# Making GpSimd's loads wait for the preceding DMA transposes, in a sliding-window attention followed by a SiLU MLP

## The chip, the cores and the metric

The kernel runs on one core of a Trainium2 chip. The metric is device time in microseconds (us), median of several executions. An execution over 1.5% above the fastest of its kernel is called slow, the others fast. Ratios use fast executions alone; medians are over all. A profile is one execution. Its times count from the start of its span.

## The reference, cut to what matters

```python
# q, k, v: (8 batches, 8 heads, 576 positions, 64), float32
scores = q @ k.T / 8
# heads 0-3: plain window of 32 positions; heads 4-7: every 4th of 128
attn = softmax(where(mask, scores, -1e9))
x = (attn @ v) -> (4608 tokens, 512)
h = x @ w_in                    # 512 -> 2048
out = (h * sigmoid(h)) @ w_out  # 2048 -> 512
```

The MLP takes most of TensorE's time: 9 groups of 512 tokens, each with a part `h` (x times w_in) and a part `y` (times w_out). A group needs the attention of one more batch than the group before it (the last group excepted).

## The kernel before

Batches 0 and 1 are transposed on TensorE. For batches 2 to 7, the route of q and k is: GpSimd issues a DMA that casts them to fp16 in DRAM (`kq_s`, `issue_cast`); SyncE issues four DMA transposes that read `kq_s` and write `nat` (heads 0-3) and `kqT` (heads 4-7) in SBUF (`issue_turn`; the four for batch b are called "step b" below); TensorE makes the scores; the attention output goes to DRAM (`x_s<-oP`, `x_s<-oD`, SyncE) and comes back through one more DMA transpose (`xA<-x_s` or `xR<-x_s`, SyncE) as the input of `h`. The output stores (`out_dram<-ob`; `ob` is a buffer that `y` is copied to) are in SyncE's queue as well. GpSimd also loads v (`vraw`, `vp`).

```python
def issue_cast(b):                       # GpSimd queue
    for i, src in enumerate((k, q)):
        nc.gpsimd.dma_start(out=kq_s[b][i]..., in_=src[b]...)

def issue_turn(b):                       # SyncE queue: "step b"
    ...
    for i in range(2):                   # nat: overlapping windows, 2304 x 128
        nc.sync.dma_start_transpose(out=dst[:, None, :], in_=win)
    for i in range(2):                   # kqT
        nc.sync.dma_start_transpose(out=kqTs[b % 2][:, i], in_=rows)

def issue_v(b):                          # GpSimd queue: vraw twice, vp once
    ...

def turn_gen(b):
    issue_turn(b)
    yield "DMA", max(12.0, ARRIVE.get(b, (0.0,))[0] - plan.now)

def group_gen(g):
    ...
    nc.sync.dma_start_transpose(out=x_of(g)[:, :, GT - n :], in_=x_s[t0 : t0 + n])
    yield "DMA", 6.0

# in attention(b):
if kind == "S" and b + 2 < B:            # after the last scores of batch b: step b + 2
    st.after = lambda: count(("S", b), NS,
        lambda: plan.push(turned[b + 2], turn_gen(b + 2), plan.t))
if kind in "PD":                         # after the last attn @ v of batch b
    def loads():
        if b + 2 < B: issue_v(b + 2)
        if b + 3 < B: issue_cast(b + 3)
    st.after = lambda: count(("V", b), NB + 2 * DIL, loads)
```

The program is put in order at build time by a small planner (`plan`). The numbers in `yield "DMA", us` and in `ARRIVE` are its guesses of when data will be there. They delay nothing on the chip; they only shape the order of instructions in each engine's queue. Each queue runs in order.

The softmax here doesn't subtract the row's maximum and nothing guards it: scores larger than these inputs give would overflow.

## Time and profile before

| before | |
|---|---|
| time | 400.66 us, median of 2 runs (399.76 to 401.56) |
| PE busy | 310.9 us of 399.8, 78% |
| PE busy in 260-400 us | 39.7 of 40, then 95.9 of 100 us |
| PE busy in 66-102 us | 7.5 of 36 us |
| PE busy in 160-190 us | 9.4 of 30 us |

The profile page: busy time per engine, then the span in 40 slices of 10 us. A digit is the busy share in tenths. PEclk is the clock granted to TensorE in tenths, GB/s is what the DMA engines moved.

```profile
span 399.8 us, 5645 instructions
PE 310.9 (78%) x2200; PEld 148.8 (37%) x2200; DVE 200.4 (50%) x477; ACT 153.4 (38%) x258; POOL 45.7 (11%) x64
PE   0679985060898099900999499999999999999996
PEclk9999999557799689975799979999999999999999
GB/s 118 192 201 206 192 161 151 85 162 89 196 205 207 153 35 133 127 92 190 21 153 179 176 128 180 147 84 58 78 67 59 126 75 26 26 54 26 28 79 79
```

PE has holes at slices 7-10, 13-14, 18-19 and 23 (counted from 1), and is full from slice 24, 230 us, on. So TensorE is the limit late in the kernel, and something else is the limit early. The waits view says what ended each idle stretch (columns: who waited and for whom, us in total, times, longest us):

```profile
PE h L602 <- DMA xR<-x_s: 26.9, 2, 20.7
ACT ob L641 <- DMA out_dram<-ob: 23.1, 2, 15.9
PE s L402 <- DMA nat<-kq_s: 17.6, 1, 17.6
PE y L630 <- ACT ob L641: 11.1, 2, 10.9
PE h L602 <- DMA xA<-x_s: 9.6, 1, 9.6
```

PE's four lines add up to 65 us. Every one ends with a DMA that SyncE issues: a step (`nat`), an x transpose, or an output store that frees `ob`. SyncE's timeline, cut to steps 2 and 4 and what follows them (start us, duration us, merged instructions with their count; a merged line covers the waits in it):

```profile
50.71 23.83 SPq L130 DMA_TRANSPOSE nat<-kq_s  x2
74.58 12.03 SPq L134 DMA_TRANSPOSE kqT<-kq_s  x2
86.66 0.58 SPq L642 DMA_DIRECT2D out_dram<-ob  x1
...
113.53 13.72 SPq L130 DMA_TRANSPOSE nat<-kq_s  x2
127.35 2.89 SPq L134 DMA_TRANSPOSE kqT<-kq_s  x2
130.34 2.69 SPq L475 DMA_DIRECT2D x_s<-oD  x2
136.87 1.44 SPq L297 DMA_TRANSPOSE xA<-x_s  x1
```

A step holds the queue for 36 us (50.7 to 86.6) or 17 us (113.5 to 130.2). What stands behind it goes out at its end: the first output store at 86.66, the last stores of batch 2's attention at 130.34. Only then can `xA` be transposed, and `h` of group 2 starts at 140.3.

Why is a step so slow? The DMA view of the stretch 68-80 us, in the middle of step 2 (q1 is SyncE's queue, q0 GpSimd's; packets, MB, share of 16 engines' time; times of packets overlap, so shares can add to over 100%):

```profile
DMA packets 4361, 1.08 MB, mean 90 GB/s; under 512 B 3918, under 2 KB 4361, under 8 KB 4361
q1 hardware_dynamic: 2155, 0.55, 99.4%
q0 software_dynamic: 2206, 0.54, 81.5%
```

Two queues share the engines, about equally in bytes, and together move 90 GB/s. The same view of 20-28 us, when only GpSimd's queue moves data:

```profile
DMA packets 2235, 1.62 MB, mean 202 GB/s; under 512 B 62, under 2 KB 2233, under 8 KB 2233
```

And of 216-220 us, when nearly only transposes run:

```profile
DMA packets 3597, 0.91 MB, mean 228 GB/s; under 512 B 3565, under 2 KB 3597, under 8 KB 3597
```

### The profile page before, as it was taken

The page shows a single profiled execution, that of the slowest core. Times are in us where ns is not written, and L with a number is a line of the kernel's source. Part 1 is how long each engine was busy: PE and PEld are TensorE (multiplying, and loading weights), DVE is VectorE, ACT ScalarE, POOL GpSimd, SP SyncE. Part 2 cuts the span into 40 slices and gives each one's busy share as a digit, 9 for nine tenths or more (in the row PEclk, how much of TensorE's full clock was granted, in tenths as well). Part 3 has the DMA queues.
Part 4 walks back from the last instruction along what each step waited for, and adds up shares of the span by engine and source line. Part 5 has one row for each costly group of instructions (what it writes and reads, how often), then busy time and mean ns, then how long its engine had stood idle before and what let it go on. Part 6 is the DMA issues. An engine that isn't in the chain of part 4 may idle for free.

```text
span 399.8 us, 5645 instructions
## 1 busy us (share of the span) xinstructions
PE 310.9 (78%) x2200; PEld 148.8 (37%) x2200; DVE 200.4 (50%) x477; ACT 153.4 (38%) x258; POOL 45.7 (11%) x64
## 2 busy tenths in 40 slices
PE   0679985060898099900999499999999999999996
PEld 0553443020343044400444144444444444444442
DVE  6584696020687058600585358577568625425300
ACT  1554750000555055500455144544555425435311
POOL 8525312000020011000020010000000000000000
PEclk9999999557799689975799979999999999999999
DMA  9999999999999919998099949621311610010022
GB/s 118 192 201 206 192 161 151 85 162 89 196 205 207 153 35 133 127 92 190 21 153 179 176 128 180 147 84 58 78 67 59 126 75 26 26 54 26 28 79 79
DMA packets 115898, 47.41 MB, mean 119 GB/s; under 512 B 82592, under 2 KB 111264, under 8 KB 115872
## 3 DMA queue, kind: packets, MB, share of 16 engines
q0 software_dynamic: 47152, 19.92, 43.3%
q1 hardware_dynamic: 68720, 27.14, 40.9%
q8 instruction: 17, 0.28, 0.3%
q14 instruction: 9, 0.07, 0.1%
HBM read 39.84 MB, written 20.05 MB: 150 GB/s over the span
## 4 chain that ended last, share of the span: by engine, by line
PE 64%; DMA 12%; SPq 11%; DVE 8%; ACT 2%; issue 1%; POOL 1%; ACTq 0%; POOLq 0%
PE h L602 29%; PE y L630 28%; SPq L134 6%; SPq L130 5%; DMA out_dram<-ob 4%; DMA x_s<-oD 3%; DMA xR<-x_s 3%; PE s L402 2%; DMA nat<-in_q_dram 2%; DVE oD L442 2%; PE av_d L438 2%; DVE gT L613 2%; DVE oP L442 1%; PE av_p L438 1%; DVE probs L417 1%
## 5 line engine op out<-in xcount | busy, mean ns | idle before, releaser
L630 PE MATMUL y<-w_out,gT 128*128 128x512 f16 x576 | 142.7, 387 | 11.7 <-ACT ob L641 11.1
L613 DVE SCALAR_TENSOR_TENSOR gT<-th,h 128x512 f16<-128x512 f32 x144 | 98.1, 683 | 89.9 <-ACT th L611 89.8
L611 ACT ACTIVATE th<-h 128x512 f32<-128x512 f32 x144 | 86.1, 598 | 121.6 <-PE h L602 114.4
L602 PE MATMUL h<-xR,w_in 128*128 128x512 f16 x384 | 95.5, 389 | 26.9 <-DMA xR<-x_s 26.9
L602 PEld LDWEIGHTS <-w_in 128*128 128x128 f16 x576 | 54.9, 100 | 101.8 <-issue 48.4
L630 PEld LDWEIGHTS <-gT 128*128 128x128 f16 x576 | 54.4, 99 | 73.5 <-issue 15.8
L602 PE MATMUL h<-xA,w_in 128*128 128x512 f16 x192 | 51.1, 401 | 11.4 <-DMA xA<-x_s 9.6
L410 ACT ACTIVATE probs<-s 128x768 f16<-128x768 f32 (+2 forms) x45 | 36.4, 808 | 35.6 <-PE s L402 35.6
L641 ACT ACTIVATE ob<-y 128x512 f32<-128x512 f32 x36 | 21.5, 598 | 69.0 <-PE y L630 45.9
L438 PEld LDWEIGHTS <-probs 128*128 128x128 f16 x448 | 23.6, 102 | 15.4 <-issue 1.5
L417 DVE TENSOR_TENSOR probs<-probs,mask_p 128x768 f16<-128x768 f16 x24 | 13.3, 553 | 31.3 <-ACT probs L410 30.9
L442 DVE TENSOR_TENSOR oD<-av_d,rcps 72x256 f16<-72x256 f32 x64 | 26.9, 421 | 2.2
L441 DVE RECIPROCAL rcps<-av_p 96x4 f32<-96x4 f32 x48 | 8.4, 175 | 36.9 <-PE av_p L438 36.6
L140 POOL DMA_DIRECT2D vraw<-in_v_dram x16 | 10.9, 681 | 110.1 <-DVE vd L429 93.2
L442 DVE TENSOR_TENSOR oP<-av_p,rcps 96x256 f16<-96x256 f32 x48 | 20.2, 421 | 1.6
L402 PE MATMUL s<-nat 64*128 64x96 f16 x144 | 7.0, 224 | 17.6 <-DMA nat<-kq_s 17.6
L154 POOL DMA_DIRECT2D vp<-in_v_dram x8 | 11.5, 1436 | 70.7 <-PE av_p L438 65.6
L438 PE MATMUL av_d<-vd,probs 128*128 128x65 f16 x256 | 16.4, 199 | 1.0 <-DVE rcps L441 0.6
L438 PE MATMUL av_p<-vp,probs 128*128 128x65 f16 x192 | 13.8, 205 | 1.5 <-DVE probs L417 0.9
L417 DVE TENSOR_TENSOR probs<-probs,mask_d 128x864 f16<-128x864 f16 (+1 forms) x24 | 13.2, 549 | 1.7 <-ACT probs L410 1.4
L402 PEld LDWEIGHTS <-nat 64*128 64x128 f16 x144 | 4.2, 103 | 25.9 <-issue 25.9
L372 PE MATMUL td<-ident,nat 96*128 96x96 f16 x48 | 4.3, 242 | 11.1 <-DMA nat<-in_k_dram 7.0
(59 smaller groups left out, 117.2 us busy)
## 6 DMA issues: line engine op xcount, KB each, us to landing
out_dram<-ob SPq DMA_DIRECT2D x36, 256.0 KB, 2.7
kq_s<-in_k_dram POOLq DMA_DIRECT2D x6, 576.0 KB, 18.6
kq_s<-in_q_dram POOLq DMA_DIRECT2D x6, 576.0 KB, 21.0
vp<-in_v_dram POOLq DMA_DIRECT2D x7, 384.0 KB, 14.5
w_in<-in_moe_w_in_dram POOLq DMA_DIRECT2D x4, 512.0 KB, 12.4
w_out<-in_moe_w_out_dram POOLq DMA_DIRECT2D x4, 512.0 KB, 16.5
vraw<-in_v_dram POOLq DMA_DIRECT2D x8, 224.0 KB, 9.0
x_s<-oP SPq DMA_DIRECT2D x12, 144.0 KB, 2.7
```

Source lines behind the costliest of these rows:

```text
L130: nc.sync.dma_start_transpose(out=dst[:, None, :], in_=win)
L134: nc.sync.dma_start_transpose(out=kqTs[b % 2][:, i], in_=rows)
L402: nc.tensor.matmul(sp[i][:, w * n : w * (n + 1)], lhs, rhs, start=True, stop=True)
L410: nc.scalar.activation(p2, both[:, :, :n], AF.Exp, scale=scale)
L417: nc.vector.tensor_tensor(p2, p2, mk, ALU.mult)
L438: nc.tensor.matmul(a[:, i, : D + 1], lhs(i), rhs(i), start=True, stop=True)
L442: nc.vector.tensor_tensor(o, a[:n, :, :D], rcp[:n, :, None].broadcast_to([n, HN, D]), ALU.mult)
L602: nc.tensor.matmul(h, w_in16[:, c, f * P : (f + 1) * P], x_g[:, c], start=(c == 0), stop=(c == HP - 1),)
L611: nc.scalar.activation(th, h, AF.Tanh, scale=0.5)
L613: nc.vector.scalar_tensor_tensor(gTs[g][:, f], th, 1.0, h, ALU.add, ALU.mult)
L630: nc.tensor.matmul(y, gTs[g][:, f, tb * P : (tb + 1) * P], w_out16[:, f], start=(f == 0), stop=(f == NFF - 1),)
L641: nc.scalar.activation(ob, y, AF.Copy, scale=0.5)
```

## The change

Its intent is to keep the loads of v and the casts out of the way of the transposes. Two GpSimd copies read the last column of each `kqT` of step b. GpSimd's queue runs in order, so the loads behind these copies are issued only when the step has landed. Steps 2 and 3 are also given later planned times, and a few guesses of the planner are changed.

```diff
+    fence = cpool.tile([P, 2], F16, name="fence")
...
-    ARRIVE = {0: (8.5, 15.0), 1: (33.0, 47.0), 2: (60.0, 60.0), 3: (75.0, 75.0)}
+    ARRIVE = {0: (8.5, 15.0), 1: (33.0, 47.0), 2: (60.0, 70.0), 3: (80.0, 90.0)}
+    TURN_AT = {2: 51.0, 3: 72.0}
...
     def turn_gen(b):
+        yield "DMA", max(0.0, TURN_AT.get(b, 0.0) - plan.now)
         issue_turn(b)
-        yield "DMA", max(12.0, ARRIVE.get(b, (0.0,))[0] - plan.now)
+        count(("L", b - 2), 2, lambda: loads_after(b))
+        yield "DMA", 9.0
+
+    def loads_after(b):
+        for i in range(2):
+            nc.gpsimd.tensor_copy(fence[:, i : i + 1], kqTs[b % 2][:, i, 1, HN * M - 1 :])
+        issue_v(b)
+        if b + 1 < B:
+            issue_cast(b + 1)
...
-        yield "DMA", 6.0                     # group_gen
+        yield "DMA", 8.0
...
-                def loads():
-                    if b + 2 < B:
-                        issue_v(b + 2)
-                    if b + 3 < B:
-                        issue_cast(b + 3)
-
-                st.after = lambda: count(("V", b), NB + 2 * DIL, loads)
+                if b + 2 < B:
+                    st.after = lambda: count(
+                        ("V", b), NB + 2 * DIL,
+                        lambda: count(("L", b), 2, lambda: loads_after(b + 2)),
+                    )
```

## The prediction

> **What bounds the kernel now.** TensorE, but only after about 230 us. Page: PE busy 310.9 us of 399.8. Windows view: PE busy 29.6 of 30 us in 230-260, 39.7 of 40 in 260-300, 95.9 of 100 in 300-400; that tail can't shrink. The loss is earlier. The waits view lists five PE waits ended by a DMA or by what one held up: `s<-nat` 17.6 us (to 83.6), `y` behind `ob`, whose buffer waits for an output store, 10.9 (to 101.5), `h<-xA` 9.6 (to 140.3), `h<-xR` 20.7 (to 190.1) and 6.2 (to 230.4). Together 65 us.
>
> **Their cause.** SyncE's timeline shows the four transposes of a step taking, first issue to last, 36 us (step 2), 21, 17, 31, 18, then 12 (step 7). Nothing later in that queue can start before them: the x_s<-oD stores of the batch two earlier go out at 130.3, 180.9 and 220.8, within 0.1 us of a step's last transpose. The slow steps are those with GpSimd's v loads and casts in flight. DMA view: alone, casts move about 200 GB/s (20-28 us), transposes 228 (216-220); together 90 (68-80) and 99 (88-100). The Trainium skill, "DMA: Bandwidth & Descriptors", section "Issuing engines are not separate DMA queues", says queues interleave on the same 16 DMA engines; the trace agrees, and adds that the sum halves.
>
> **What the change does.** Two tiny GpSimd copies per step (estimate 0.1-0.3 us each, from the other small GpSimd instructions; off the critical path) read the transposes' last column, so v(b) and casts(b+1) start only when step b has landed. Transposes 2 and 3 move back in SyncE's queue. No byte is saved.
>
> Estimates: 1.77 MB of transposes per step at 220 GB/s plus landing, 10 us. 1.95 MB (v and casts) at 200 GB/s plus issue and landing, 16 us (15 at 199-214). They now alternate, 27 us per step, less than TensorE's 35.
>
> Casts 2 land at 53.5 as before, so transposes 2 land near 62, casts 3 near 78, transposes 3 near 88, casts 4 near 104-108; transposes 4 finish near 114-120 (130.2 before). What follows collides: x_s<-oD and the x transpose now always run against the just released v and casts. At the 40-60 GB/s that transposes got in company, that adds about 7 us to the 9.5 seen from last transpose to `h`. Group 2's `h` starts near 131 (140.3 before), group 3's near 160-167 (190.1), group 4's near 195-205 (230.4); the remaining 169.5 us follow unchanged. Of 65 us of waits 30-35 remain: 20-30 before group 2, where TensorE has run out of work, and small ones later.
>
> **Predicted: 366 us, 8 in 10 between 350 and 384.** Faster by over 2%: 0.92; within 2%: 0.05; slower by over 2%: 0.03.
>
> **What would show it right.** Each step's transposes take 8-13 us of SyncE's queue, with neither v nor casts in flight. `s<-nat` waits under 5 us, `h<-xR` under half of 26.9; `h<-xA` stays or grows (10-30). New: GpSimd waits for kqT. PE is dense from about 205 us; its busy time falls a little (300-310), with fewer restarts at a low granted clock.
>
> **What would make it wrong.** Output stores stuck behind a transpose that waits for its later casts, stalling `y`: the alternation is a serial chain and can pass 30 us per step. x transposes slowed by over 7 us. Or an x path less disturbed than I think: then near 354. A late step 7 starving groups 5 or 6.

## The result, and the profile after

The kernel after takes 354.0 us (median of 2 runs, 353.42 to 354.58). The ratio to the kernel before is 0.8835 (95% interval 0.873 to 0.894). A ratio here is the mean time of one kernel's fast runs over that of the other's in the same rounds, so not quite the ratio of the medians. Run again later with five rounds, it took 354.1 us (ratio 0.8953, 0.890 to 0.901).

The page after (slices are 8.8 us now):

```profile
span 352.8 us, 5672 instructions
PE 305.7 (87%) x2200; PEld 148.0 (42%) x2200; DVE 201.7 (57%) x477; ACT 153.5 (44%) x258; POOL 48.2 (14%) x76
PE   0678998992987199789998999999999999999995
PEclk9999999997899579989999999999999999999999
GB/s 111 188 205 201 196 190 201 128 192 187 194 199 142 165 233 197 151 163 86 210 156 224 235 172 144 19 123 41 87 64 149 61 0 30 61 30 30 61 82 67
```

PE's work is the same 2200 matmuls. Two holes (slices 10 and 14, counted from 1) are left of four, and PE is nearly full from slice 19, 160 us, on. The waits view after, the same kinds of line:

```profile
POOL fence L300 <- DMA kqT<-kq_s: 142.8, 12, 31.6
PE h L611 <- DMA xA<-x_s: 10.2, 1, 10.2
ACT ob L650 <- DMA out_dram<-ob: 9.8, 1, 9.8
PE y L639 <- ACT ob L650: 8.1, 5, 6.6
PE h L611 <- DMA xR<-x_s: 4.3, 2, 3.2
```

The wait of `s` for `nat` (17.6 us) is gone; `h` for `xR` fell from 26.9 to 4.3; PE's lines add up to 22.6 us instead of 65. These 43 us and the 5 us by which PE's busy time fell (310.9 to 305.7) account for about the 47 us by which the span fell. GpSimd now idles 142.8 us at the fence, which costs nothing in itself: what it holds back there is the loads, as meant. SyncE's timeline after, the same places:

```profile
49.77 6.33 SPq L131 DMA_TRANSPOSE nat<-kq_s  x2
56.15 2.90 SPq L135 DMA_TRANSPOSE kqT<-kq_s  x2
59.10 0.58 SPq L651 DMA_DIRECT2D out_dram<-ob  x1
...
98.87 5.82 SPq L131 DMA_TRANSPOSE nat<-kq_s  x2
104.80 3.48 SPq L135 DMA_TRANSPOSE kqT<-kq_s  x2
108.37 1.92 SPq L486 DMA_DIRECT2D x_s<-oD  x2
112.59 2.40 SPq L308 DMA_TRANSPOSE xA<-x_s  x1
```

Step 2 starts within a microsecond of where it did (49.8 against 50.7) but holds the queue for 9.3 us instead of 35.9. All six steps take 9.0 to 9.4 us. The DMA view of 54-60 us, the middle and end of step 2:

```profile
DMA packets 4088, 1.03 MB, mean 171 GB/s; under 512 B 4088, under 2 KB 4088, under 8 KB 4088
q1 hardware_dynamic: 4088, 1.03, 108.4%
```

No packet of GpSimd's queue is in it. Of 66-72 us, when v and casts run without transposes:

```profile
DMA packets 3663, 1.03 MB, mean 172 GB/s; under 512 B 3040, under 2 KB 3662, under 8 KB 3662
```

So the same kinds of load and transpose that moved 90 GB/s together move 172 and 228 alone. In the longer stretch 50-102 us the DMA engines moved 127 GB/s before (6.62 MB) and 179 GB/s after (9.29 MB): more of the same work got done in the same time. The difference is in SyncE's queue alone: it moved 2.30 MB before and 5.07 after, GpSimd's 4.28 and 4.17.

One thing did not happen. The prediction says that transposes 2 and 3 move back in SyncE's queue. The instruction lists of the two builds show the same order at the head of that queue: step 2, one output store, step 3, two output stores. A build of the kernel after without `TURN_AT` has the same sequence on SyncE and GpSimd as the one with it, and not on TensorE, ScalarE and VectorE, where batch 2's scores stand earlier. It was not run, so what `TURN_AT` alone is worth is not shown; run 2 below tests the planner's numbers as a whole. What these change is the order on TensorE, ScalarE and VectorE and the place of later stores.

### The profile page after: what moved, and what is told of

Read it like the earlier page. It is cut to its first block, busy times and chain, and to the rows that moved or that the text cites. A ratio compares the mean times of both kernels' runs of the same rounds, so it can differ in the third digit from the quotient of the medians.

```text
span 352.8 us, 5672 instructions
## 1 busy us (share of the span) xinstructions
PE 305.7 (87%) x2200; PEld 148.0 (42%) x2200; DVE 201.7 (57%) x477; ACT 153.5 (44%) x258; POOL 48.2 (14%) x76
## 4 chain that ended last, share of the span: by engine, by line
PE 73%; DMA 14%; DVE 6%; ACT 4%; SPq 1%; issue 1%; POOL 1%; ACTq 0%; POOLq 0%
PE h L611 33%; PE y L639 32%; DMA xR<-x_s 5%; DMA xA<-x_s 3%; DMA x_s<-oD 3%; PE s L413 2%; DMA nat<-in_q_dram 2%; PE av_d L449 2%; DVE oD L453 1%; PE av_p L449 1%; DVE gT L622 1%; SPq L135 1%; ACT th L620 1%; DVE oP L453 1%; ACT ob L650 1%; ACT probs L421 1%
## 5 line engine op out<-in xcount | busy, mean ns | idle before, releaser
L639 PE MATMUL y<-w_out,gT 128*128 128x512 f16 x576 | 141.0, 383 | 8.5 <-ACT ob L650 8.1
L611 PE MATMUL h<-xR,w_in 128*128 128x512 f16 x384 | 93.7, 383 | 4.4 <-DMA xR<-x_s 4.3
L639 PEld LDWEIGHTS <-gT 128*128 128x128 f16 x576 | 53.6, 98 | 68.5 <-issue 10.2
L611 PE MATMUL h<-xA,w_in 128*128 128x512 f16 x192 | 51.2, 404 | 13.3 <-DMA xA<-x_s 10.2
L453 DVE TENSOR_TENSOR oD<-av_d,rcps 72x256 f16<-72x256 f32 x64 | 26.9, 421 | 2.2
L300 POOL COPY fence<-kqT 128x1 f16<-128x1 f16 x12 | 2.4, 202 | 142.8 <-DMA kqT<-kq_s 142.8
L452 DVE RECIPROCAL rcps<-av_d 72x4 f32<-72x4 f32 x64 | 11.0, 172 | 5.0 <-PE av_d L449 4.9
## 6 DMA issues: line engine op xcount, KB each, us to landing
w_out<-in_moe_w_out_dram POOLq DMA_DIRECT2D x4, 512.0 KB, 16.5
```

The lines of the kernel that those rows point to most:

```text
L452: nc.vector.reciprocal(rcp[:n], a[:n, :, D : D + 1])
L453: nc.vector.tensor_tensor(o, a[:n, :, :D], rcp[:n, :, None].broadcast_to([n, HN, D]), ALU.mult)
L611: nc.tensor.matmul(h, w_in16[:, c, f * P : (f + 1) * P], x_g[:, c], start=(c == 0), stop=(c == HP - 1),)
L639: nc.tensor.matmul(y, gTs[g][:, f, tb * P : (tb + 1) * P], w_out16[:, f], start=(f == 0), stop=(f == NFF - 1),)
```

## The experiments

Theory A: loads and transposes in flight together cost each other time, and the wait keeps them apart. Rival B: the gain comes from the planner's new numbers and the orders that follow from them. All runs gave correct results. Runs 1 to 4, 5 to 8, 9 and 10, and 11 and 12 shared a chip and rounds.

| run | median us | ratio to before (95%) |
|---|---|---|
| 1 wait only | 361.1 | 0.905 (0.897-0.913) |
| 2 no wait | 394.3 | 0.983 (0.973-0.993) |
| 3 loads wait for x too | 350.7 | 0.881 (0.876-0.887) |
| 4 casts before v | 364.2 | 0.916 (0.910-0.922) |
| 5 stores before step 3 | 354.1 | 0.893 (0.888-0.899) |
| 6 x before the step | 337.3 | 0.850 (0.845-0.855) |
| 7 x before the step, no wait | 367.8 | 0.927 (0.922-0.933) |
| 8 runs 5 and 6 together | 334.6 | 0.844 (0.837-0.851) |
| 9 only casts wait | 371.1 | 0.933 (0.925-0.941) |
| 10 only v waits | 358.1 | 0.898 (0.889-0.906) |
| 11 kernel after again | 354.1 | 0.895 (0.890-0.901) |
| 12 run 5 again | 355.6 | 0.899 (0.895-0.904) |

### 1. The wait alone

```diff
  # the kernel before, plus `fence`, `loads_after` and its two counts; no TURN_AT,
  # and ARRIVE, 12.0 and 6.0 as before
     def turn_gen(b):
         issue_turn(b)
+        count(("L", b - 2), 2, lambda: loads_after(b))
         yield "DMA", max(12.0, ARRIVE.get(b, (0.0,))[0] - plan.now)
```

> The kernel before with nothing added but the wait: GpSimd's loads of v and casts start once the step's transposes have landed; the planner's numbers and the order on TensorE, ScalarE, VectorE and SyncE are those of before, instruction for instruction. Theory A (loads and transposes halve each other's rate, the wait keeps them apart): 352 to 362 us, each step's transposes issued in 8 to 12 us. Rival B (the gain comes from the planner's new numbers and the order that follows from them): 390 to 402 us.

361.1 us. The six steps take 8.8 to 9.7 us. The order on the four other engines is that of the kernel before, instruction for instruction, so no rival that works through their order can explain this gain. ("The four other engines" are all but GpSimd.)

### 2. Everything but the wait

```diff
     def loads_after(b):
-        for i in range(2):
-            nc.gpsimd.tensor_copy(fence[:, i : i + 1], kqTs[b % 2][:, i, 1, HN * M - 1 :])
         issue_v(b)
```

> The kernel after without the two fence copies, so all of its orders and planner numbers but no wait. Theory A: 390 to 405 us, the step 2 transposes again take over 25 us of SyncE's queue, together with loads at about 90 GB/s in sum. Rival B: 352 to 362 us.

394.3 us over all four executions; by its two fast ones 1.7% under before (interval 0.7 to 2.7%, so neither clearly the same nor clearly 2% faster), where the wait alone gives 9.5%. The product of the two ratios, 0.9048 x 0.9829 = 0.889, lies between the two ratios measured for the whole change (0.8835, 0.8953), so the runs fit a wait and an order that simply add up. Step 2 in SyncE's timeline is as slow as before:

```profile
50.00 21.06 SPq L130 DMA_TRANSPOSE nat<-kq_s  x2
71.10 13.34 SPq L134 DMA_TRANSPOSE kqT<-kq_s  x2
```

The stretch 50-102 us moves 137 GB/s, near the 127 of before and far from the 179 of after. Rival B is left with some 2%.

### 3. Holding the loads until x has passed

In the kernel after, the loads released by step b + 2 meet batch b's last x_s stores and its x transpose. Here they are held for that too.

```diff
     def loads_after(b):
         for i in range(2):
             nc.gpsimd.tensor_copy(fence[:, i : i + 1], kqTs[b % 2][:, i, 1, HN * M - 1 :])
+        for g in [g for g in range(NG) if b - 2 >= PEB and need[g] == b - 2]:
+            nc.gpsimd.tensor_copy(fence[:, 2:3], x_of(g)[:, 0, GT - 1 :])
  # and a third count, given by group_gen after its transpose
```

> The kernel after, with the loads of batches 4 to 7 held a little longer, until the x transpose of the batch two earlier has landed too. Theory A says that the x transposes, 10 us each now, are slowed by the loads released at the same moment: they should take 3.5 to 5 us, and group 2's first matmul should start 5 to 7 us sooner (near 116). Later steps start later by as much, so in total between 346 and 354 us. If the x transposes are slow for another reason (their own size, output stores), they stay near 10 us and the total grows to 355 to 362.

350.7 us. The tile view of `xA` gives the time from issue to landing. In the kernel after:

```profile
DMA to landing us min/median/max: 10.0/10.0/10.0
```

In this run:

```profile
DMA to landing us min/median/max: 3.6/3.6/3.6
```

So the x transpose is slowed by the loads and not by its size. Group 2's `h` starts at 118.7 instead of 122.6 us, a gain of 4 us where 5 to 7 were expected. About 1% of the total is won (350.7 against 354.1, though not of the same rounds). The next step starts 3 us later (130.9 against 127.9), which may be why it is no more.

### 4. Casts before v

```diff
     def loads_after(b):
         ...
-        issue_v(b)
         if b + 1 < B:
             issue_cast(b + 1)
+        issue_v(b)
```

> The kernel after, with the casts of the next step put before the loads of v in GpSimd's queue. The next transposes wait for the casts alone, so they now start some 5 us sooner, while v is still in flight. If what matters is how soon the casts land (rival C: the serial chain of casts and transposes), each step is 4 to 5 us shorter and group 2 starts near 113, total 344 to 350. Theory A: the transposes then run against v, take 12 to 20 us instead of 9.5, and nothing or less is gained: 353 to 366.

364.2 us, slower than the kernel after. Step 3 does start 6 us sooner, at 67.6, and ends where it did (82.7 against 83.3 us), as it takes 15 us instead of 9:

```profile
67.61 11.94 SPq L131 DMA_TRANSPOSE nat<-kq_s  x2
79.60 3.07 SPq L135 DMA_TRANSPOSE kqT<-kq_s  x2
```

An earlier start against other traffic gave nothing here, and v came later: PE now waits 6.6 us for `vp`, and 10.5 in all for `xR`.

### 5 and 12. Output stores ahead of step 3

The kernel after still shows `y` waiting 6.6 us for `ob`, whose store stands behind step 3 in SyncE's queue, and step 3 itself waits for its casts. Is that a part of the critical path?

```diff
+        def go():
+            issue_turn(b)
+            count(("L", b - 2), 2, lambda: loads_after(b))
+        if b == 3: held.append(go)      # issued after the third output store
+        else: go()
```

> The kernel after, with output stores 2 and 3 ahead of the step 3 transposes in SyncE's queue; orders on TensorE, ScalarE and VectorE unchanged. Those transposes wait for casts until 74 us while the two outputs are ready at 62 and 68, so nothing is delayed. The wait of y for ob (6.6 us before 86.5) should go. Theory A with the serial chain: group 2 still cannot start before its x has passed step 4 in SyncE's queue, so it starts at 121 to 124 as before, its wait grows by 5 to 7 us, and the total stays at 351 to 355. If TensorE's own work set the time there, the total falls by 5 to 7 us, to 346 to 349.

> The two output stores ahead of the step 3 transposes once more, now beside the kernel after. If the wait for ob was off the critical path, both agree within 0.7%. If it was on it, this one is 5 to 7 us faster.

It is not. The two lines of the waits view in run 5:

```profile
PE h L619 <- DMA xA<-x_s: 17.0, 1, 17.0
PE y L647 <- ACT ob L658: 1.5, 4, 0.7
```

The wait for `ob` is gone (8.1 to 1.5 us in total) and the wait for `xA` has grown by as much (10.2 to 17.0): group 2 starts at 121.3, in the kernel after at 122.6. The profile of run 5 is of its slowest execution (358.7 us, the others 353.7 to 355.1); that of run 12, at 355.5 us, shows the same two waits, 1.5 and 17.6. In run 12, beside the kernel after in run 11, the total is 355.6 against 354.1 us. Run 11:

> The kernel after, unchanged, on the same chip and in the same rounds as the next run, since it had only two runs so far: 352 to 357 us.

### 6. x before the step

If x standing behind step b + 2 is what holds TensorE, then issue x first. Step 4 is not urgent: its scores come only after all of group 2's `h`.

```diff
     def group_gen(g):
         ...
         nc.sync.dma_start_transpose(out=x_of(g)[:, :, GT - n :], in_=x_s[t0 : t0 + n])
+        b = need[g] + 2
+        if b < B and turned[b].done is None:
+            plan.push(turned[b], turn_gen(b), plan.now)
         yield "DMA", 8.0
...
-            if kind == "S" and b + 2 < B:
+            if kind == "S" and b < PEB:      # steps 4 to 7 no longer start here
```

> The kernel after, with steps 4 to 7 issued only once the x transposes of the batch two earlier are in SyncE's queue, instead of ahead of its last x_s stores. Theory: what still holds group 2 (10.2 us) and 3 (3.2 us) is x standing behind a step's transposes and then running against the loads that those release. With x first, group 2's x should be there at 106 to 111, its wait under 2 us, and the x transposes should take 3.5 to 5 us: 334 to 344 us in total. If the late landing of the casts itself were what holds TensorE, the gaps would only move to the scores of batch 4 (s waiting for nat), and the total would stay within 350 to 356.

337.3 us, 5% under the kernel after. SyncE's timeline around step 4:

```profile
97.72 6.01 SPq L489 DMA_DIRECT2D x_s<-oD  x2
105.78 1.43 SPq L308 DMA_TRANSPOSE xA<-x_s  x1
107.31 1.38 SPq L654 DMA_DIRECT2D out_dram<-ob  x1
108.79 4.81 SPq L131 DMA_TRANSPOSE nat<-kq_s  x2
```

`xA` is issued at 105.8 instead of 112.6 us, in front of step 4. No wait of `h` for `xA` or `xR`, and none of `s` for `nat`, is left in the waits view, and `h` of group 2 starts at 114.1. One part of the expectation missed: later x transposes still meet loads (5.4 to 12.7 us from issue to landing), but by then TensorE has other work.

### 7. The same order without the wait

The edit of run 6, put into the kernel before.

> The same order of SyncE's queue put into the kernel before, without any wait of the loads for the transposes. If head-of-line blocking alone is the cost, this gets most of the gain without the wait: 345 to 362 us. Theory A: steps 2 and 3 still take 36 and 20 us against the loads, group 2 starts near 130, and later transposes still lose; 365 to 385 us, so better than before, but behind the wait alone.

367.8 us. The order alone is worth 7%, less than the wait alone (9.5%). Steps 2 and 3 still take 34.7 and 21.2 us, and PE still waits 16.1 us for `nat` and 16.5 for `ob`. So head-of-line blocking (an item that waits because a long one stands before it in its queue) is not the whole cost, and the wait is needed as well.

### 8. Both orders and the wait

The edits of runs 5 and 6 together, on the kernel after.

> e5 and e6 together. With x first, TensorE's own work is what ends last, so now the 6.6 us that e5 takes away should count: 3 to 7 us under e6, 329 to 339 us. If x is late in e6 for any other reason, it equals e6.

334.6 us (332.5 to 337.1) is the best, but its interval overlaps that of run 6, so what the stores add is not clear of noise (2.7 us between the medians, just under the 3 to 7 that were expected). TensorE is now 91% busy:

```profile
span 331.6 us, 5665 instructions
PE   0568998999879996999999999999999999999995
PEclk9999999999989999999999999999999999999999
```

### 9 and 10. Which load does the harm?

```diff
  # run 9: issue_v(b + 2) goes back to the end of batch b's attention, only casts wait
  # run 10: issue_cast(b + 3) goes back there, only v waits
```

> The kernel after, but only the casts wait for the transposes; the loads of v (small packets of 128 bytes for the most part) start as soon as their buffers are free, as in the kernel before. Orders on the other engines unchanged. Which load is it that the transposes suffer from? If both kinds: a step that meets v takes 14 to 17 us as in the run with the casts first, total 356 to 368. If the casts alone: steps take 9 to 11 us, and as fewer bytes are left to load between two steps the total is 344 to 352.

> The other half: only v waits, the casts start as early as in the kernel before. If the casts are the main cause: steps that meet casts take 18 to 35 us and the total is 370 to 392. If v were the main cause: steps of 9 to 12 us, total 345 to 356.

Both kinds do, but both totals missed what I expected, in opposite directions. With v free (371.1 us) steps start when they did in the kernel after (49.8, 73.7, 99.1, 126.7) and take 15.2 to 16.6 us, so all of the x path comes 6 to 7 us later. With casts free (358.1 us) the four early steps take 14.3 to 20.8 us, but they no longer wait for their casts: step 3 starts at 65.1 instead of 73.8 and ends at 82.8, where it ended anyway (83.3). An early start pays for the slower step. (This run does not keep v and transposes quite apart: v(2) waits for step 2, but step 3 then starts at once and meets both v(2) and the next casts.) In the stretch 50-102 us the two runs move 175 and 191 GB/s, like the 179 of the kernel after. So with half of the wait the total rate is whole; a step is slow there because it shares. The total itself falls, to 127, 137 and 138, only in the kernel before and in runs 2 and 7, the three without any wait, where GpSimd has issued the loads of v(2), v(3), casts 3 and casts 4 before step 2 is through.

## Why the prediction was right

The measured 354.0 us is in the range (350 to 384), at its fast end, 12 us under the central value. Point by point:

- **What bounds the kernel.** Right. The tail is nearly unchanged: from the start of group 4's `h` to the end took 169.4 us before (399.8 - 230.4) and 165.6 after (352.8 - 187.2). These 4 us are a part of the miss: TensorE was busy for 160.7 us of it instead of 165.1, with 24 fewer matmuls left to do and a granted clock of 1.00 instead of 0.98.
- **The cause, steps slowed by loads.** Right: run 1 gives most of the gain with nothing but the wait, run 2 shows that little is left without it. "The sum halves" holds where it was read (90 GB/s, against 172 for v and casts and 228 for transposes alone; the "casts" of 20-28 us in the text were the weights, so its figure of 200 was of another load) but is too general: runs 9 and 10 keep 175 and 191 GB/s over 50-102 us with part of the loads beside the transposes. The Trainium skill, "DMA: Bandwidth & Descriptors", section "Issuing engines are not separate DMA queues", speaks of interleaving; that part the runs bear out: a step that shares takes 14 to 21 us instead of 9.
- **"Transposes 2 and 3 move back in SyncE's queue."** Wrong, but it carried no weight: the queue's order there is the same in both builds.
- **"10 us per step, 16 us for the loads, 27 us for both."** The step was right (9.0 to 9.4 us). The whole was too long, and this is the main term that was mis-sized: steps 2, 3 and 4 start at 49.8, 73.8 and 98.9 us, 24 to 25 us apart. The first `nat` transpose needs the cast of k alone: step 3 starts 12 us after the first v load is issued (61.8), while the cast of q lands only at 76.6. I had added up times that overlap. (So a cast is still in flight in the first 2.8 us of step 3; "neither v nor casts in flight" holds for the rest of it.)
- **Group 2 near 131, group 3 at 160-167, group 4 at 195-205.** Measured 122.6, 151.4 and 187.2 us: each about 8 us or more early. Of that, 6 us or more come from step 4, whose last transpose ended at 108.3 and not at 114 to 120.
- **The collision of x with the released loads.** Right in kind. `xA` took 10.0 us to land, and 3.6 when the loads were held (run 3). From the last transpose of step 4 to `h` took 14.3 us (108.3 to 122.6), where I expected 16.5.
- **The gap before group 2, 20 to 30 us.** 10.2 us measured. Run 5 shows that 17 us would have stood there, had PE not lost 6.6 us at `ob` first. Of the 65 us of waits 22.6 remain, not 30 to 35.
- **"Output stores stuck behind a transpose that waits for its later casts."** It happened (6.6 us of `y`) and cost nothing, as group 2 waited for x anyway (runs 5, 11 and 12).
- **PE busy 300 to 310 us, fewer restarts at a low clock.** 305.7 us. The Trainium skill, "TensorE: Matmul & The Clock Gate", section "Part 1: The HAM clock gate", says that an idle TensorE falls to half its clock and needs some 3.4 us of work to come back. The trace agrees: before, the granted clock is 0.50 in the idle 72-80 us and still 0.50 in 101.5-105.1, after another wait, where 8 `y` matmuls took 3.57 us (8 at 128.9 us took 1.89); over 105-110 us it is 0.91. After, the mean clock of the span is 0.966 instead of 0.914.

The text also says "then near 354" for a less disturbed x path. That this number was hit is luck: the x path was only 2 us quicker than expected, and most of the 12 us came from the shorter time between steps (24 to 25 us, not 27) and the tail.

The expected gain was not lost, then, but it was not all that this idea had in it: 17 us more lay in the order of SyncE's queue (run 6), which neither kernel had touched.

What stays open: why the total DMA rate falls to 127 GB/s over 50-102 us in the kernel before, 137 in run 2 and 138 in run 7, and not in runs 9 and 10, where loads and transposes also overlap, but with fewer loads queued at once; and why all of it is lost in SyncE's queue. The runs show that it does, not by what mechanism.

## What to carry to other kernels

If a profile shows two streams of DMAs at once and their sum below what each moves alone, let the less urgent one wait for the other: a tiny copy of the last landed element, on the engine that issues the loads, is enough. Then look at what the wait now releases, and at what stands behind the slow DMA in the same queue: an item that the critical path needs belongs in front of a long one that nobody needs yet. Before mending a wait, ask which wait comes next in line: the 6.6 us taken away in run 5 came back whole in the next one.

## What the Trainium skill lacked or had wrong

- "DMA: Bandwidth & Descriptors", section "Rules for kernel authors", says that a transpose beside ordinary DMAs needs nothing. For correct results the runs agree; for time it lacks the cost: a step of four transposes took 9.0 to 9.4 us alone, 14 to 21 us beside part of the loads (runs 9 and 10, early steps), up to 36 us in the kernel before, and the DMA engines moved 127 instead of 179 GB/s over the same 52 us.
- The same page, section "Issuing engines are not separate DMA queues", calls the sequencer's time to issue a DMA usually small relative to the DMA. For DMA transposes it was not: in the kernel after each `kqT` transpose held SyncE's queue for 1.3 to 2.3 us and landed 3.2 to 3.4 us after its issue. A step held the queue for 9 us at best and 36 us at worst, and everything behind it waited.
